# Retention attention in pairs of tiles, with eight tiles of loads ahead

## The chip, the cores and the metric

The kernel runs on one core of a Trainium2 chip. The metric is the device time of one execution in microseconds (us), lower is better; the time before is 1463.5 us, the median of three runs between 1459.63 and 1469.09. The core has five engines that run their own queues of instructions in order: TensorE (PE, matmuls and weight loads), VectorE (DVE), ScalarE (ACT), GpSimd (POOL) and SyncE (SP, which mostly issues DMAs). ACT and POOL issue DMAs too.

## The reference

```python
# _attn_ref: 8 batches, 8 heads, 576 positions, head size 64
scores = scale * np.matmul(q, k.transpose(0, 1, 3, 2))
Dmat = np.where(rel >= 0, gamma[:, None, None] ** rel[None, :, :], 0.0)
return np.matmul(scores * Dmat[None, :, :, :], v)
...
# _moe_ref: x is the attention's output as 4608 rows of 512
logits = x @ w_gate + modality_bias[modality_id]
e_idx = np.argmax(logits, axis=1)
...                                   # gate_w: softmax weight of the chosen expert
out[mask] = gate_w[mask, None] * (np.maximum(x[mask] @ w1[e], 0.0) @ w2[e])
...
# _moe2_ref
h = x @ w_in
return (h - np.tanh(h)) @ w_out
```

## The kernel before

The work has three stages: attention with routing (the first 165 us or so), the experts, and the second feed-forward layer. The change touches only the first, and the place in SBUF of the second layer's weights.

**Attention.** The 4608 rows are cut into 36 tiles of 128 rows. A batch has 576 rows, so nine tiles (PERIOD) hold two batches, and the fifth tile of nine holds the end of one and the start of the next. Within a tile all pairs of positions are computed with a mask; what comes from earlier tiles of the same batch goes through a running state. Per tile there are four groups of matmuls on PE, and each uses the array in another form, which the rows show as partitions of input x output: the scores, keys times queries (L301, 64*128); the state times the queries (L337, 64*64); the values times the masked scores (L345, 128*64); and the keys times the values, added to the state (L360, 128*64). Tiles without an earlier one in their batch have no state-times-query.

**Around it.** DVE multiplies the scores by the mask (L305, two instructions a tile, each frees one of three PSUM banks `sc`) and takes the sum `xp` out of PSUM with the decay factors `gx` (L370). ACT copies the state out (L364), POOL scales the values (L311, `vs`). `attend` does the last three matmul groups of a tile; the loop over t issues the scores of tile t+1 first, then `attend(t)`, `evac_x(t)`, the scaling of tile t+2, and the loads of tile t+4 (AHEAD is 4). SP issues the loads `qk` and `vk`, 512 KB each; a load waits until its buffer's last reader is done.

**Routing.** Four tiles make a group. In the group's next four tiles the loop does `route_a` (gate matmuls, L401, and a copy on ACT, L404), `route_b` (four transposes, L410, and seven small DVE instructions), and `route_c` (rank matmuls, L435 to L440, then on DVE the positions from L443 and the gate to L453), one in each tile. Each tile also stores an older one: `turn_x` transposes it on PE (L468, four transposes, written `turn` below), ACT multiplies it by the gate (L473, `xo`) and issues the DMA to `x_d` (L474). POOL scatters the token numbers (L457). All of these use two PSUM banks with the name `m`; a group of matmuls that needs the third waits until the reader of the first is done. `xo` has two buffers as well, each free when its DMA has landed.

**The end of the stage.** After group 6 `due` doubles the stores of its tiles, `choose` (L376) picks the first expert, SP loads that expert's token numbers, POOL gathers its rows, PE turns them (L148), and the first expert matmul is L630.

Of the kernel before, what the change touches and what calls it, by code (L numbers as in the profile page):

```python
# [8 lines left out]
F32 = mybir.dt.float32  # L9
F32R = mybir.dt.float32r  # L10
# [4 lines left out]
ALU = mybir.AluOpType  # L15
# [9 lines left out]
TL = 128  # L25
NTILE = NT // TL
PERIOD = 9
AHEAD = 4
RG = 4
NRG = NTILE // RG  # L30
UE = 400
# [70 lines left out]
def kernel(tc, A, out):  # L102
    nc = tc.nc
    with ExitStack() as ctx:
# [9 lines left out]
        tok_d = dram.tile([NT + UE, 1], I32, name="tok_d")  # L114
        wo_d = dram.tile([F3, 128, DM], F32, name="wo_d")
        keep = pool("keep", 1)
        wres = pool("wres", 1)

        ident = keep.tile([128, 128], F32, name="ident")
        winh = wres.tile([128, F3, DM], F32R, name="winh")  # L120
        winl = wres.tile([128, F3, DM], F32R, name="winl")

        xT_p = [pool("xTa", 1), None]
        idt0 = keep.tile([128, SE], I32, name="idt0")
        pick = keep.tile([1, 2], I32, name="pick")
# [74 lines left out]
        with tc.manual_schedule():  # L200
# [3 lines left out]
            p1, p1r = pools(c1), pools(c1r)  # L204
            att = p1("att", 1)
            gld = p1("gld", AHEAD)
            tmp = p1("tmp", 2)
            const = p1r("const", 1, side="right")
            xt_p = p1r("xt", 3, side="right")
            xo_p = p1r("xo", 2, side="right")  # L210
# [6 lines left out]
            mask = att.tile([128, 2, TL], F32, name="mask")  # L217
            gx = att.tile([128, PERIOD, H // 2, TL], F32, name="gx")
            vsc = att.tile([128, PERIOD, H], F32, name="vsc")
            state = [att.tile([128, H // 2, D], F32, name=f"state{i}") for i in range(2)]  # L220
            wg = const.tile([128, KD, 32], F32, name="wg")
            ltri = const.tile([128, 128], BF16, name="ltri")
            ones = const.tile([128, 128], BF16, name="ones")
# [21 lines left out]
            def load_gx(r):  # L245
                nc.sync.dma_start(out=gx[:, r], in_=A["gx"][r])
# [11 lines left out]
            nc.scalar.dma_start(out=mb.rearrange("p a e -> p (a e)"), in_=A["mb"].to_broadcast([128, 2 * E]))  # L258
            load_tile(3)
            load_gx(2)  # L260


            nc.gpsimd.memset(ones, 1.0)
# [29 lines left out]
            def scores(t):  # L293

                qk, vk = gt[t]
                a = tmp.tile([128, 2, H // 2, TL], F32, name="a")
                sc = [ps_sc.tile([128, H // 2, TL], F32, name="sc") for _ in range(2)]
                for p in range(H // 2):
                    for s in range(2):
                        r64 = slice(64 * s, 64 * s + 64)  # L300
                        nc.tensor.matmul(out=sc[s][:, p, :], lhsT=qk[r64, 1, p, :], rhs=qk[r64, 0, p, :],  # L301
                                         start=True, stop=True, tile_position=(64 * s, 0))
                m = int(t % PERIOD == PERIOD // 2)
                for s in range(2):
                    nc.vector.tensor_tensor(out=a[:, s], in0=sc[s], in1=mask[:, m:m + 1, :].to_broadcast([128, H // 2, TL]), op=ALU.mult)  # L305
                a_t[t] = a
# [8 lines left out]

            st_box = [None]

            def attend(t):
                qk, vk = gt.pop(t)
                r = t % PERIOD  # L320
                xp = ps_x.tile([128, 2, 4, TL], F32, name="xp")
                a, vs = a_t.pop(t), v_t.pop(t)
                inter = r != 0

                mid_t = r == PERIOD // 2
                after = not inter or mid_t or t == NTILE - 1
                w = TL // 2 if mid_t else TL

                def before():

                    if inter:
                        ss = s_t.pop(t)
                        for p in range(H // 2):
                            for s in range(2):
                                c = s ^ p % 2
                                r64 = slice(64 * s, 64 * s + 64)
                                nc.tensor.matmul(out=xp[64 * c:64 * c + 64, s, p // 2, 0:w], lhsT=ss[r64, p, :], rhs=qk[r64, 0, p, 0:w],  # L337
                                                 start=not after and p < 2, stop=after, skip_group_check=True, tile_position=(64 * s, 64 * c))

                if not after:  # L340
                    before()
                for p in range(H // 2):
                    for s in range(2):
                        c = s ^ p % 2
                        nc.tensor.matmul(out=xp[64 * c:64 * c + 64, s, p // 2, :], lhsT=vs[:, 2 * p + s],  # L345
                                         rhs=a[:, s, p, :], start=after and p < 2, stop=True,
                                         skip_group_check=True, tile_position=(0, 64 * c))
                if after:
                    before()
                x_ps[t] = xp[:, :, 0:2]  # L350
                if r != PERIOD - 1:
                    first = r == 0 or mid_t
                    if first:
                        st_box[0] = ps_st.tile([128, H // 2, D], F32, name="st")
                    st = st_box[0]
                    k0 = TL // 2 if mid_t else 0
                    for p in range(H // 2):
                        for s in range(2):
                            h = 2 * p + s
                            nc.tensor.matmul(out=st[64 * s:64 * s + 64, p, :], lhsT=vk[k0:TL, 1, h * D:(h + 1) * D],  # L360
                                             rhs=vs[k0:TL, h], start=first and p == 0, stop=True, skip_group_check=True,
                                             tile_position=(k0, 64 * s))
                    s_t[t + 1] = state[t % 2]
                    nc.scalar.copy(out=state[t % 2], in_=st)  # L364

            def evac_x(t):
                g, r = divmod(t, RG)
                if r == 0:
                    xt[g] = xt_p.tile([128, KD, RG * TL], F32, name="xt")
                nc.vector.tensor_tensor(out=xt[g][:, :, r * TL:(r + 1) * TL].rearrange("p (s b) t -> p s b t", s=2), in0=x_ps.pop(t),  # L370
                                        in1=gx[:, t % PERIOD].rearrange("p (s b) t -> p s b t", s=2), op=ALU.mult)
# [104 lines left out]
            def store_x(t, spare=False):  # L476
# [4 lines left out]
            scaled(0)  # L481
            scores(0)
            scaled(1)
            bt = xo_p.tile([128, DM], F32, name="xo")
            midf, midn = bt[:, 0:NTILE], bt[:, NTILE:2 * NTILE]
            b1 = bt[:, 2 * NTILE:(2 + E) * NTILE].rearrange("p (t e) -> p t e", e=E)
            nc.gpsimd.tensor_copy(out=midf, in_=mid[:, :, 0])
            nc.gpsimd.tensor_scalar(out=midn, in0=midf, scalar1=-1.0, scalar2=1.0, op0=ALU.mult, op1=ALU.add)
            sh = [128, NTILE, E]
            nc.gpsimd.tensor_tensor(out=bias, in0=midn.unsqueeze(2).to_broadcast(sh),  # L490
                                    in1=mb[:, 0:1, :].to_broadcast(sh), op=ALU.mult)
            nc.gpsimd.tensor_tensor(out=b1, in0=midf.unsqueeze(2).to_broadcast(sh),
                                    in1=mb[:, 1:2, :].to_broadcast(sh), op=ALU.mult)
            nc.gpsimd.tensor_tensor(out=bias, in0=bias, in1=b1, op=ALU.add)
            def due(w):

                r = w - (EARLY - 1) * RG
                return [w][w < 0:] if not 0 <= r < RG else [w + r, w + r + 1] if r < RG // 2 else []

            for t in range(NTILE):  # L500
                g, r = divmod(t, RG)
                if t + 1 < NTILE:
                    scores(t + 1)
                attend(t)
                evac_x(t)
                if t + 2 < NTILE:
                    scaled(t + 2)
                if t + AHEAD < NTILE:
                    load_tile(t + AHEAD)
                if t + 3 < PERIOD:  # L510
                    load_gx(t + 3)
                if t >= RG + 3:
                    for w in due(t - RG - 3):
                        scatter(w)
                if g >= 1:
                    if r == 0:
                        ls_box[g - 1] = route_a(g - 1)
                    elif r == 1:
                        route_b(g - 1, ls_box.pop(g - 1))
                    elif r == 2:  # L520
                        route_c(g - 1)
# [3 lines left out]
                if t == (EARLY + 1) * RG - 1:  # L525
                    choose()
                if t == (EARLY + 1) * RG + 1:
# [83 lines left out]
            t_ahead = late.pop(0)  # L611
            tp_ahead = turn_x(t_ahead, False)
            c1.close()


            def blocks(names, nf, lag, width, xT, load_w, gemm1_w, gemm2, post, prep, finish):
# [341 lines left out]
```

## Time and profile before

| | |
|---|---|
| median of 3 runs | 1463.5 us (1459.63 to 1469.09) |
| profiled execution | 1468.45 us, span 1466.7 us |
| busy over the span | PE 96%, DVE 71%, ACT 47%, POOL 17% |
| busy in 30 to 145 us | PE 115.00 of 115 us, DVE 77.15, ACT 31.76, POOL 55.20 |

Engine times are busy times of one profiled execution. A wait is the idle time of an engine just before an instruction, put down to the work that ended last before it. In rows of the timeline the first column is the start in us, the second the length in us, then engine, line, operation, output and inputs, shape and count, and in square brackets the idle time before. A matmul's row ends later than the next one may start, so the spacing of starts tells what a group takes.

### The profile page before, as it was taken

How to read it: one execution, taken by the hardware profiler on the slowest of the kernel's cores; microseconds unless marked ns; L12 is line 12 of the kernel's file. 1: busy time of each engine (PE TensorE's matmuls, PEld its weight loads, DVE VectorE, ACT ScalarE, POOL GpSimd, SP SyncE). 2: the span in 40 equal slices, each digit the busy share in tenths (PEclk: the TensorE clock that was granted, in tenths of full speed). 3: DMA queues.
4: the chain of work that ended last, by engine and by line, in shares of the span. 5: the costliest groups of instructions: out<-in, count | busy, mean ns of one | idle time of the engine just before them, and what ended most of it. 6: DMA issues, size and time to landing. Idle time of an engine off the chain costs nothing.

```text
span 1466.7 us, 22476 instructions
## 1 busy us (share of the span) xinstructions
PE 1404.4 (96%) x8427; PEld 1214.1 (83%) x8427; DVE 1046.8 (71%) x1745; ACT 683.1 (47%) x1269; POOL 244.8 (17%) x304
## 2 busy tenths in 40 slices
PE   6999689899999999999989999999999999999997
PEld 5888489888999999998768888888888888888885
DVE  2666367877788887438877768777677777778764
ACT  0223144233444444336655555555555555555543
POOL 4455321111111110012420011110011110011101
PEclk8999899999999999999999999999999999999998
DMA  9999354334364443532110000000000010000000
GB/s 331 342 329 327 118 182 130 112 120 109 105 184 93 86 86 98 144 66 59 58 57 1 29 29 29 29 1 31 28 29 29 21 38 1 29 29 0 30 1 29
DMA packets 65490, 130.32 MB, mean 89 GB/s; under 512 B 22288, under 2 KB 29136, under 8 KB 65376
## 3 DMA queue, kind: packets, MB, share of 16 engines
q1 hardware_dynamic: 49168, 91.96, 21.7%
q0 software_dynamic: 7904, 21.96, 4.6%
q10 hardware_dynamic: 8304, 14.91, 2.8%
q8 instruction: 68, 1.11, 0.3%
q14 instruction: 46, 0.38, 0.1%
HBM read 130.97 MB, written 35.61 MB: 114 GB/s over the span
## 4 chain that ended last, share of the span: by engine, by line
PE 42%; issue 6%; DVE 4%; ACT 1%; POOL 1%; DMA 1%; DVEq 0%; POOLq 0%; ACTq 0%
PE hp L630 21%; PE acc L915 7%; PE acc L916 7%; PE acc L917 7%; DVE xl L896 1%; DVE xl L897 1%; DMA o<-wo_d 1%; ACT xh L886 1%; DVE xh L888 1%; DVE xl L895 1%; POOL out_dram L928 0%; DVE lo L891 0%; POOL woutl L869 0%; ACT xh L893 0%; ACT xl L894 0%
## 5 line engine op out<-in xcount | busy, mean ns | idle before, releaser
L915 PE MATMUL acc<-wouth,hi 128*128 128x512 f32 x576 | 226.1, 393 | 4.6 <-ACT o L925 4.6
L630 PE MATMUL hp<-yh,winh 128*128 128x512 f32 x576 | 226.4, 393 | 1.7 <-PEq L851 1.7
L917 PE MATMUL acc<-wouth,lo 128*128 128x512 f32 x576 | 226.1, 393 | 1.7 <-DVE lo L891 1.7
L630 PE MATMUL hp<-yl,winh 128*128 128x512 f32 x576 | 226.2, 393 | 0.0
L630 PE MATMUL hp<-yh,winl 128*128 128x512 f32 x576 | 226.1, 393 | 0.0
L916 PE MATMUL acc<-woutl,hi 128*128 128x512 f32 x576 | 226.1, 393 | 0.0
L885 ACT ACTIVATE xh<-hp 128x512 f32<-128x512 f32 x144 | 86.1, 598 | 297.1 <-PE hp L630 275.4
L887 DVE TENSOR_TENSOR xl<-xh,hp 128x512 f32<-128x512 f32 x144 | 99.0, 688 | 160.6 <-ACT xh L886 160.6
L730 ACT ACTIVATE hi<-hp 128x400 fp32r<-128x400 f32 x96 | 48.4, 505 | 224.8 <-PE hp L630 147.6
L896 DVE SCALAR_TENSOR_TENSOR xl<-xh,xl 128x512 f32<-128x512 f32 x144 | 136.7, 950 | 15.4 <-DVE xl L895 0.5
L830 PE MATMUL acc<-hi,wh 128*128 128x400 f32 x384 | 138.5, 361 | 9.5 <-DVE yo L807 8.6
L832 PE MATMUL acc<-hi,wl 128*128 128x400 f32 x384 | 134.3, 350 | 3.0 <-DVE wl L706 2.6
L630 PE MATMUL hp<-xl,wh 128*128 128x400 f32 x384 | 132.9, 346 | 0.4 <-DVE xl L150 0.4
L915 PEld LDWEIGHTS acc<-wouth,hi 128*128 128x128 f32 x576 | 108.7, 189 | 29.3 <-ACT o L925 5.0
L630 PE MATMUL hp<-xh,wl 128*128 128x400 f32 x384 | 132.7, 345 | 0.2 <-DVE wl L706 0.2
L630 PE MATMUL hp<-xh,wh 128*128 128x400 f32 x384 | 132.3, 345 | 0.2 <-ACT wh L705 0.2
L831 PE MATMUL acc<-lo,wh 128*128 128x400 f32 x384 | 132.4, 345 | 0.0
L917 PEld LDWEIGHTS acc<-wouth,lo 128*128 128x128 f32 x576 | 108.6, 189 | 28.2 <-DVE lo L891 5.2
L630 PEld LDWEIGHTS hp<-yh,winh 128*128 128x128 f32 x576 | 108.3, 188 | 26.2 <-PEq L851 2.0
L630 PEld LDWEIGHTS hp<-yh,winl 128*128 128x128 f32 x576 | 108.1, 188 | 24.8
L916 PEld LDWEIGHTS acc<-woutl,hi 128*128 128x128 f32 x576 | 108.7, 189 | 23.3
L630 PEld LDWEIGHTS hp<-yl,winh 128*128 128x128 f32 x576 | 108.1, 188 | 24.0
(162 smaller groups left out, 2544.2 us busy)
## 6 DMA issues: line engine op xcount, KB each, us to landing
raw<-in_w_dram SPq DMA_DIRECT2D x91, 512.0 KB
qk<-in_qk_dram SPq DMA_DIRECT2D x36, 512.0 KB
vk<-in_vk_dram SPq DMA_DIRECT2D x35, 512.0 KB
y_d<-yo SPq DMA_DIRECT2D x12, 800.0 KB
yr<-y_d SPq DMA_DIRECT2D x9, 1024.0 KB
raw<-in_wo_dram SPq DMA_DIRECT2D x16, 512.0 KB
raw<-in_wi_dram SPq DMA_DIRECT2D x16, 512.0 KB
x_d<-xo ACTq DMA_DIRECT2D x28, 256.0 KB
```

The costliest lines, as they stand in the source:

```text
L630: nc.tensor.matmul(out=hp, lhsT=lhs, rhs=rhs, start=j == 0, stop=j == 3 * KD - 1)
L730: nc.scalar.activation(out=hi, in_=hp, func=ACTF.Relu)
L830: nc.tensor.matmul(out=o, lhsT=wh[:, cs], rhs=hi, start=first, stop=False)
L831: nc.tensor.matmul(out=o, lhsT=wh[:, cs], rhs=lo, start=False, stop=False)
L832: nc.tensor.matmul(out=o, lhsT=wl[:, cs], rhs=hi, start=False, stop=last)
L885: nc.scalar.activation(out=u, in_=hp, func=ACTF.Square)
L886: nc.scalar.activation(out=t, in_=hp, func=ACTF.Tanh)
L887: nc.vector.tensor_tensor(out=v, in0=u, in1=hp, op=ALU.mult)
L896: nc.vector.scalar_tensor_tensor(out=v, in0=s, scalar=SQ_C, in1=v, op0=ALU.add, op1=ALU.mult)
L915: nc.tensor.matmul(out=acc[s], lhsT=hi[:, c], rhs=wouth[f], start=first, stop=False)
L916: nc.tensor.matmul(out=acc[s], lhsT=hi[:, c], rhs=woutl[f], start=False, stop=False)
L917: nc.tensor.matmul(out=acc[s], lhsT=lo[:, c], rhs=wouth[f], start=False, stop=last)
```

## The change

Two tiles go through the loop together. `attend` is split into `keep_state` (keys times values and the copy of the state), `intra` (values times masked scores) and `inter` (state times queries). For a pair t, t+1 the order on PE is: scores of t+2; `keep_state(t)`, `intra(t)`, `intra(t+1)`, `keep_state(t+1)`, `inter(t)`, `inter(t+1)`; then `route_a` where it is due; scores of t+3; then the transposes of two older tiles, with `route_b` between them or `route_c` ahead of them. Both tiles of a pair share one `xp` tile of two banks, and both `evac_x` stand behind the second `inter`. Scaled values and masked scores have four buffers instead of two, the state three instead of two, the loads eight instead of four, and eight tiles of loads are issued ahead of the loop. The POOL work on the routing bias moves behind the scaling of the second pair. The weights `winh` and `winl` get their place in SBUF after attention's buffers are given up instead of ahead of them.

```diff
-AHEAD = 4
+AHEAD = 8
...
-            tmp = p1("tmp", 2)
+            tmp = p1("tmp", 4)
...
-            state = [att.tile([128, H // 2, D], F32, name=f"state{i}") for i in range(2)]
+            state = [att.tile([128, H // 2, D], F32, name=f"state{i}") for i in range(3)]
...
+            for t in range(4, AHEAD):
+                load_tile(t)
+                load_gx(t - 1)
...
-            for t in range(NTILE):
+            for t in range(0, NTILE, 2):
                 g, r = divmod(t, RG)
-                if t + 1 < NTILE:
-                    scores(t + 1)
-                attend(t)
-                evac_x(t)
-                if t + 2 < NTILE:
-                    scaled(t + 2)
...
+                if t + 2 < NTILE:
+                    scores(t + 2)
+                keep_state(t)
+                intra(t)
+                intra(t + 1)
+                keep_state(t + 1)
+                inter(t)
+                inter(t + 1)
+                evac_x(t)
+                evac_x(t + 1)
+                for w in (t + 2, t + 3):
+                    if w < NTILE:
+                        scaled(w)
...
+                if g >= 1 and r == 0:
+                    ls_box[g - 1] = route_a(g - 1)
+                if t + 3 < NTILE:
+                    scores(t + 3)
+                if g >= 1 and r == 0:
+                    out_tiles(t)
+                    route_b(g - 1, ls_box.pop(g - 1))
+                    out_tiles(t + 1)
+                elif g >= 1:
+                    route_c(g - 1)
+                    out_tiles(t)
+                    out_tiles(t + 1)
```

Here `out_tiles` does a tile's scatters and stores. Two places of the order follow. First PE at a tile with the ranks (`route_c`), from one scores to the next; before, where a tile has one store (`sc` scores, `st` keys times values, `m` the shared banks, a bracket names the engine waited for):

```order
L337 MATMUL xp<-qk,state_122 64x128 x7
L345 MATMUL xp<-a,vs 64x128 [waits Pool_49]
L345 MATMUL xp<-a,vs 64x128 x7
L360 MATMUL st<-vs,vk 64x64 [waits DMAHW2_49]
L360 MATMUL st<-vs,vk 64x64 x7
L468 MATMUL m<-ident,xt 128x128 [waits DVE_49]
L468 MATMUL m<-ident,xt 128x128 x3
L301 MATMUL sc<-qk 128x128 [waits DMAHW7_49]
```

That is the tile after the ranks: the bank that the ranks' reader on DVE must free is asked for one whole tile later. The same work in the changed kernel, in the second pair of a group:

```order
L365 MATMUL xp<-qk,state_117 64x128 x8
L365 MATMUL xp<-qk,state_118 64x128 x8
L300 MATMUL sc<-qk 128x128 [waits DMAHW0_49]
L300 MATMUL sc<-qk 128x128 [waits DVE_49]
L300 MATMUL sc<-qk 128x128 x6
...
L442 MATMUL m<-cum,ones 128x32
L470 MATMUL m<-ident,xt 128x128 x4
L470 MATMUL m<-ident,xt 128x128 [waits DVE_49]
L470 MATMUL m<-ident,xt 128x128 x3
L300 MATMUL sc<-qk 128x128 [waits DMAHW2_49]
```

Now the second transpose stands four transposes behind the ranks and waits for DVE. Then DVE around the ranks' reader `rk`; before:

```order
L305 TENSOR_TENSOR a<-sc,mask 128x512 x2
L370 TENSOR_TENSOR xt<-xp,gx 128x4x128
L443 TENSOR_TENSOR rk<-m,ecap 128x32
L444 TENSOR_TENSOR rk<-rk,oh_all 128x32
L446 TENSOR_REDUCE pos_s<-rk 128x4
```

And in the changed kernel:

```order
L304 TENSOR_TENSOR a<-sc,mask 128x512 x2
L372 TENSOR_TENSOR xt<-xp,gx 128x4x128 x2
L304 TENSOR_TENSOR a<-sc,mask 128x512 x2
L445 TENSOR_TENSOR rk<-m,ecap 128x32
L446 TENSOR_TENSOR rk<-rk,oh_all 128x32
```

The reader of the ranks stood behind one evacuation, and now stands behind two evacuations and two masks that come after them.

## Rows read from the trace of the kernel before

**Rows 1.** Windows: busy us (count) by engine, granted PE clock, DMA share, GB/s
```profile
20.00:30.00 10.00, 5.67 (x64) 5.05 (x64) 1.79 (x3) 0.00 (x0) 4.54 (x7) 0.50 1.03 402
30.00:145.00 115.00, 115.00 (x1977) 94.31 (x1975) 77.15 (x192) 31.76 (x65) 55.20 (x77) 0.99 0.94 330
```

**Rows 2.** Timeline of PE alone, one tile from scores to scores
```profile
109.19 0.19 PE L435 MATMUL m<-oh_all,ltri 128*128 128x32 bf16 x1
...
109.33 0.63 PE L468 MATMUL m<-ident,xt 128*128 128x128 f32 x4
109.89 1.16 PE L301 MATMUL sc<-qk 64*128 64x128 f32 x16
110.98 0.67 PE L337 MATMUL xp<-qk,state 64*64 64x128 f32 x16
111.58 1.09 PE L345 MATMUL xp<-a,vs 128*64 128x128 f32 x16
112.50 0.64 PE L360 MATMUL st<-vs,vk 128*64 128x64 f32 x16
113.07 0.66 PE L468 MATMUL m<-ident,xt 128*128 128x128 f32 x4
113.66 0.38 PE L301 MATMUL sc<-qk 64*128 64x128 f32 x2
```

**Rows 3.** Waits in the first 200 us: us, times, longest
```profile
PE sc L301 <- DMA qk<-in_qk_dram: 10.1, 2, 5.7
PE xp L345 <- POOL vs L311: 4.0, 1, 4.0
PE m L376 <- ACT xo L473: 3.6, 1, 3.6
```

**Rows 4.** Waits of SP's DMA queue, first 200 us
```profile
SPq L241 <- PE xp L337: 57.5, 25, 3.7
SPq L242 <- PE st L360: 29.8, 20, 4.4
```

**Rows 5.** Timeline, tiles 30 and 31 and the stores behind them
```profile
141.48 1.09 PE L468 MATMUL m<-ident,xt 128*128 128x128 f32 x8
...
141.67 0.19 DVE L443 TENSOR_TENSOR rk<-m,ecap 128x32 f32<-128x32 f32 x1
...
142.50 0.97 PEld L301 LDWEIGHTS sc<-qk 64*128 64x128 f32 x16 [0.17 <-issue]
...
143.70 1.29 DVE L305 TENSOR_TENSOR a<-sc,mask 128x512 f32<-128x512 f32 x2
143.74 0.69 ACT L473 ACTIVATE xo<-m,gate 128x512 f32<-128x512 f32 x1 [1.90 <-DVE se L451]
144.46 0.33 ACTq L474 DMA_DIRECT2D x_d<-xo  x1
...
149.50 0.69 ACT L473 ACTIVATE xo<-m,gate 128x512 f32<-128x512 f32 x1 [2.79 <-DMA x_d<-xo]
150.22 0.33 ACTq L474 DMA_DIRECT2D x_d<-xo  x1
150.24 0.17 PE L376 MATMUL m<-cum,ones 128*128 128x8 bf16 x1 [3.59 <-ACT xo L473]
```

**Rows 6.** Groups by line, first 200 us: busy us, mean ns, idle before
```profile
L370 DVE TENSOR_TENSOR xt<-xp,gx 128x512 f32<-128x512 f32 x36 | 24.8, 690 | 25.7 <-PE xp L345 14.3 <-remote 7.7 <-DMA gx<-in_gx_dram 2.9
L473 ACT ACTIVATE xo<-m,gate 128x512 f32<-128x512 f32 x28 | 19.1, 683 | 23.5 <-DVE se L452 7.4 <-DMA x_d<-xo 6.1 <-PE sc L301 3.8
```

**Rows 7.** Timeline at the end of the stage, last tile to first expert
```profile
165.53 0.67 PE L337 MATMUL xp<-qk,state 64*64 64x128 f32 x16
...
174.93 0.69 DVE L370 TENSOR_TENSOR xt<-xp,gx 128x512 f32<-128x512 f32 x1 [7.68 <-remote]
...
180.02 0.45 PE L630 MATMUL hp<-xh,wh 128*128 128x400 f32 x1 [0.23 <-ACT wh L705]
```

More of the change, by code (lines that the diff above doesn't have):

```diff
@@ L116 @@
         keep = pool("keep", 1)
-        wres = pool("wres", 1)
         ident = keep.tile([128, 128], F32, name="ident")
-        winh = wres.tile([128, F3, DM], F32R, name="winh")
-        winl = wres.tile([128, F3, DM], F32R, name="winl")
         xT_p = [pool("xTa", 1), None]
@@ L316, with intra @@
             st_box = [None]
[L318 to L341, printed above, removed]
+            xps = [None]
+            def intra(t):
+                if t % 2 == 0:
+                    xps[0] = ps_x.tile([128, 2, 4, TL], F32, name="xp")
+                xp = xps[0][:, :, 2 * (t % 2):2 * (t % 2) + 2]
+                a, vs = a_t.pop(t), v_t[t]
                 for p in range(H // 2):
@@ L345, in attend, with keep_state @@
                         nc.tensor.matmul(out=xp[64 * c:64 * c + 64, s, p // 2, :], lhsT=vs[:, 2 * p + s],
-                                         rhs=a[:, s, p, :], start=after and p < 2, stop=True,
+                                         rhs=a[:, s, p, :], start=t % 2 == 0 and p < 2, stop=True,
                                          skip_group_check=True, tile_position=(0, 64 * c))
-                if after:
-                    before()
-                x_ps[t] = xp[:, :, 0:2]
+                x_ps[t] = xp
+            def keep_state(t):
+                vk, vs = gt[t][1], v_t[t]
+                r = t % PERIOD
+                mid_t = r == PERIOD // 2
                 if r != PERIOD - 1:
@@ L362, in attend, with inter @@
                                              tile_position=(k0, 64 * s))
-                    s_t[t + 1] = state[t % 2]
-                    nc.scalar.copy(out=state[t % 2], in_=st)
+                    s_t[t + 1] = state[t % 3]
+                    nc.scalar.copy(out=state[t % 3], in_=st)
+            def inter(t):
+                qk = gt.pop(t)[0]
+                v_t.pop(t)
+                if t not in s_t:
+                    return
+                ss = s_t.pop(t)
+                w = TL // 2 if t % PERIOD == PERIOD // 2 else TL
+                for p in range(H // 2):
+                    for s in range(2):
+                        c = s ^ p % 2
+                        r64 = slice(64 * s, 64 * s + 64)
+                        nc.tensor.matmul(out=x_ps[t][64 * c:64 * c + 64, s, p // 2, 0:w], lhsT=ss[r64, p, :], rhs=qk[r64, 0, p, 0:w],
+                                         start=False, stop=True, skip_group_check=True, tile_position=(64 * s, 64 * c))
             def evac_x(t):
@@ L483, with make_bias @@
             scaled(1)
[L484 to L494, printed above, removed]
+            scores(1)
+            def make_bias():
+                bt = xo_p.tile([128, DM], F32, name="xo")
+                midf, midn = bt[:, 0:NTILE], bt[:, NTILE:2 * NTILE]
+                b1 = bt[:, 2 * NTILE:(2 + E) * NTILE].rearrange("p (t e) -> p t e", e=E)
+                nc.gpsimd.tensor_copy(out=midf, in_=mid[:, :, 0])
+                nc.gpsimd.tensor_scalar(out=midn, in0=midf, scalar1=-1.0, scalar2=1.0, op0=ALU.mult, op1=ALU.add)
+                sh = [128, NTILE, E]
+                nc.gpsimd.tensor_tensor(out=bias, in0=midn.unsqueeze(2).to_broadcast(sh),
+                                        in1=mb[:, 0:1, :].to_broadcast(sh), op=ALU.mult)
+                nc.gpsimd.tensor_tensor(out=b1, in0=midf.unsqueeze(2).to_broadcast(sh),
+                                        in1=mb[:, 1:2, :].to_broadcast(sh), op=ALU.mult)
+                nc.gpsimd.tensor_tensor(out=bias, in0=bias, in1=b1, op=ALU.add)
             def due(w):
@@ L498, in due, with out_tiles @@
                 return [w][w < 0:] if not 0 <= r < RG else [w + r, w + r + 1] if r < RG // 2 else []
-            for t in range(NTILE):
-                g, r = divmod(t, RG)
-                if t + 1 < NTILE:
-                    scores(t + 1)
-                attend(t)
-                evac_x(t)
-                if t + 2 < NTILE:
-                    scaled(t + 2)
[L508 to L511, printed above, removed]
+            def out_tiles(t):
                 if t >= RG + 3:
@@ L514 @@
                         scatter(w)
[L515 to L521, printed above, removed]
+                if t >= RG:
                     for w in due(t - RG - 2):
@@ L524 @@
                             store_x(w)
-                if t == (EARLY + 1) * RG - 1:
+            for t in range(0, NTILE, 2):
+                g, r = divmod(t, RG)
+                if t + 2 < NTILE:
[11 more added lines that the diff above has]
+                        scaled(w)
+                if t == 2:
+                    make_bias()
+                for w in (t, t + 1):
+                    if w + AHEAD < NTILE:
+                        load_tile(w + AHEAD)
+                    if w + AHEAD - 1 < PERIOD:
+                        load_gx(w + AHEAD - 1)
+                if g >= 1 and r == 0:
[10 more added lines that the diff above has]
+                    out_tiles(t + 1)
+                if t + 1 == (EARLY + 1) * RG - 1:
                     choose()
-                if t == (EARLY + 1) * RG + 1:
+                if t == (EARLY + 1) * RG:
                     base = nc.sync.value_load(pick[0:1, 0:1], min_val=0, max_val=(E - 1) * CAP)
@@ L613 @@
             c1.close()
+            wres = pool("wres", 1)
+            winh = wres.tile([128, F3, DM], F32R, name="winh")
+            winl = wres.tile([128, F3, DM], F32R, name="winl")
             def blocks(names, nf, lag, width, xT, load_w, gemm1_w, gemm2, post, prep, finish):
```

## The prediction, made before the changed kernel ran

> **What bounds the kernel now.** Three stages follow each other, and the change lies in the first, so I read the windows of that stage, then PE's timeline, then the waits. Between 30 and 145 us PE is busy all the time, with DVE at two thirds and ACT at a quarter [rows 1]. PE hardly waits for data there: in the whole stage it waits twice for a load, 10.1 us in all, once for the scaled values, 4.0 us, all before 30 us [rows 3]. The loads wait for PE instead: SP stood 57.5 us for the readers of `qk` and 29.8 us for those of `vk` [rows 4]. So PE's own order sets the pace, and a deeper queue of loads meets no wait in that stretch. The DMA share is 0.94 there [rows 1]; if that is a real limit, a faster PE could gain at most 0.06 x 115 = 6.9 us before loads became the bound.
>
> "Busy" hides something in PE's row. One tile takes 113.66 - 109.89 = 3.77 us [rows 2], in five groups of matmuls with four changes of the array's form: 64\*128, 64\*64, 128\*64 twice (values, then state), 128\*128. A transpose group of four takes 113.66 - 113.07 = 0.59 us of that tile. Eight transposes in a row take 1.09 us [rows 5] where four take 0.66 [rows 2], so four without a change cost 0.43. The difference, 0.16 us, is my price of one change of form; the bounds are 0 (the gap belongs to a wait that every group has) and 0.17, the idle time of the weight-load row of the next scores [rows 5].
>
> The Trainium skill has two rules on such gaps. "TensorEngine Tiling (Array Packing)", section Tiling Modes, says that a change of tiling mode drains TensorE; by that rule the pairing saves what I count below. "Perfetto Trace Analysis", section Identifying Performance Opportunities, says that the same gap repeating on the engine that should be saturated can mean too few buffers in SBUF or PSUM; by that rule the gaps stay, which is rival 3.
>
> **The change, part by part.**
> - *Forms.* Two tiles had eight changes. The new order (scores, state, values twice, state, state-times-query twice, scores, transposes) has five. Three fewer in each of 15 pairs that also store or nearly so: 45 x 0.16 = 7.2 us less (0 to 7.7).
> - *The ranks' bank.* In the second pair of each group the ranks take one of the two `m` banks, the first transpose the other, and the second transpose needs the ranks' bank back. DVE frees it after two evacuations (2 x 0.69 [rows 6]), two masks (1.29 [rows 5]) and the reader itself (0.19 [rows 5]): 2.86 us after the last state-times-query. PE gets there after a change (0.16), the scores (109.89 to 110.98, 1.09), the ranks (109.19 to 109.33, 0.14) and one transpose group (0.43): 1.82 us [rows 2]. PE waits 1.04 us, seven times: 7.3 us more. If DVE takes the first evacuation 0.44 us earlier it is 0.6 (4.2 us); with 0.3 us of hand-overs 1.3 (9.4 us). Before, a whole tile lay between. Behind PE in that wait stands everything of the next pair.
> - *The scaling's bank.* In the first pair of a group the second transpose needs the bank that ACT's scaling of the first one frees. ACT takes 0.68 us [rows 6] plus the tail of a matmul, about 0.66 - 0.43 = 0.2; only the four transposes of `route_b` lie between, 0.43. That is 0.45 us, six times: 2.7 us more (0 to 4).
> - *The gate.* From the ranks' reader (141.67) to the end of the scaling that needs the gate (143.74 + 0.69) it is 2.76 us [rows 5]. The state copy of the next pair stands behind two such scalings on ACT, and the second `keep_state` waits for it. It comes about in time; I take 1 us in all (0 to 4).
> - *Four stores at once.* At tiles 30 and 31 four tiles are stored, now in one pair. The third transpose waits for the first's scaling, which waits for the gate: 2.67 + 2.76 = 5.4 us after the last state-times-query, where PE arrives at 2.86 + 0.43 = 3.3. That is 2.1 us more (0 to 3). The wait of `choose`, 3.59 us behind the scaling that waits for a store's DMA [rows 5], stays.
> - *The start.* Up to 25 us the order of the loads is the same. The clock was 0.50 between 20 and 30 us, and the DMA share was 1.03 at 402 GB/s [rows 1], so earlier issue brings nothing there. The 4.0 us wait for scaled values [rows 3] goes, since POOL's bias work moves behind them; in its place PE waits for the scores' data of tile 4, which the new order asks for before it works on tile 2. I take 0, bounds -4 and +4.
> - *The end of the stage.* The last pair adds nothing; the first weights of the expert no longer wait for the last evacuation. But the last state-times-query starts at 165.53, and the evacuation that needs it at 174.93 after 7.68 us of idle time whose releaser the profile doesn't name; the first expert matmul is at 180.02 [rows 7]. No row tells why. I leave this wait as it is (0), and its going is rival 2. The place of `winh` and `winl` in SBUF costs nothing: they are written long after, in the experts' stage.
>
> Transferred bytes, DVE's and ACT's work and the number of matmuls are unchanged. The sum is -7.2 + 7.3 + 2.7 + 1.0 + 2.1 = +5.9 us. After the stage PE is nearly full to the end, so the shift goes through. Against the profiled execution, 1468.45 us, that is 1474; the profiled one is 5 us above the median of the three runs, and against the median I forecast 1463.5 + 5.9, about **1470 us**.
>
> **The rivals.**
> 1. *The banks come free in time.* If DVE takes the ranks' reader before PE gets there, only the fewer changes are left: -7.2 + 1.0 = -6, some 1457 us, at most the 6.9 us that the DMA share leaves. For it: DVE has a third of its time free [rows 1]. Against it: the order on DVE is fixed, and the masks need the scores that PE has just done.
> 2. *The unexplained wait at the hand-over goes.* It is 7.7 us [rows 7], and nothing in the program's order demands it. With the rest as forecast: 1470 - 7.7 = 1462 us; with rival 1 as well: 1457 - 7.7 = 1449, the only case I see near 1% faster.
> 3. *The gaps are waits, not forms.* Then the 7.2 us don't come: 1470 + 7 = 1477 us. Against it: between values and state, which have one form, PE starts the state 0.92 us after the values, no more than those take, though both sides wait on semaphores [rows 2].
> 4. *The slower side: the stores.* `xo` has two buffers, and a store took about 149.50 - 144.46 = 5.0 us from its issue to the next use of its buffer, with 2.79 us of waiting [rows 5]. Now two stores go out together, the gate-held ones at about 5.5 us after the last state-times-query; the next pair's first store wants the buffer 8.2 + 2.9 - 5.5 = 5.6 us later (a pair's time, then the gate matmuls, scores and one transpose). Four loads in a burst share the DMA engines with them. Up to 5.6 us nothing happens; at 7 us ACT waits 1.4 us six times and 2 us at `choose`, PE's transposes behind it: 1470 + 10 = 1480 us.
>
> **How the numbers follow.** The forecast has a chance of 0.50, with its own range of 1463 to 1477 from the bounds of the waits. Rival 1 has 0.20, rival 2 alone 0.08 and with rival 1 0.04, rival 3 0.06, rival 4 0.12. About 1% (14.6 us) is what a measurement of this kernel tells from no change: faster means below 1449, slower above 1478. Slower takes most of rival 4, part of rival 3 and a little of the forecast's upper end, 0.17. Faster is rivals 1 and 2 together, and a bit for what I don't see, 0.06. The rest, 0.77, is no change. The range goes from rival 1 with a gain of 8 us at the start or the end to rival 4 with a little more, 1455 to 1482 us.
>
> **What the profile after would show.** Right: on PE's timeline, starts of the four groups of a pair with fewer gaps; among the waits a new row, transposes into `m` waiting for DVE's ranks' reader, about 1 us seven times, and for ACT's scaling, about 0.5 us six times; SP waiting for PE as before; the last state-times-query some 5 to 8 us later than 165.5. Wrong: no such wait rows and an earlier end (rival 1); the evacuation of the last tile right behind its matmuls (rival 2); a tile's time in the stretch without route work still 3.8 us (rival 3); ACT's scaling waiting for `x_d` DMAs in most groups (rival 4). PE waiting for `qk` or `vk` after 35 us would break the first part: then loads, not PE, set the pace.

## The result, and the profile after

The changed kernel takes **1470.7 us** (median of 6 runs, 1466.9 to 1475.2), the kernel before beside it 1463.2 us; the ratio is 1.0058, with a 95% interval of 1.0036 to 1.0079. The forecast was 1470. The total was right by luck: the profile shows that two errors cancel in it. Attention lost 16.5 us where 5.9 were forecast, and the hand-over to the experts, forecast to stay as it was, became 9 us shorter. The profiled execution has a span of 1473.0 us, 6.3 more than before.

The same window of the changed kernel (columns as in [rows 1]):

```profile
30.00:145.00 115.00, 102.77 (x1726) 84.94 (x1724) 63.28 (x163) 26.74 (x55) 49.50 (x71) 0.98 0.88 322
```

PE, busy for all of the 115 us before [rows 1], now stands idle for 12.2 of them, at nearly the same clock (0.98 after 0.99) and with DMA less busy (0.88 after 0.94): PE waits more, and in that window not for loads (the four waits in the first row below all lie before 30 us). The longest waits of PE, and ACT's wait for its stores, in the first 200 us (us in all, times, longest):

```profile
PE sc L300 <- DMA qk<-in_qk_dram: 14.7, 4, 5.5
PE m L470 <- ACT xo L475: 6.6, 7, 2.0
ACT xo L475 <- DMA x_d<-xo: 6.4, 6, 2.0
PE m L470 <- DVE rk L445: 6.3, 7, 0.9
```

The second and the fourth row are the two that the prediction named. PE's timeline through the second pair of a group shows how they arise:

```profile
86.83 1.10 PE L365 MATMUL xp<-qk,state 64*64 64x128 f32 x32
87.86 1.16 PE L300 MATMUL sc<-qk 64*128 64x128 f32 x16
...
89.09 0.64 PE L470 MATMUL m<-ident,xt 128*128 128x128 f32 x4
90.63 0.66 PE L470 MATMUL m<-ident,xt 128*128 128x128 f32 x4 [0.91 <-DVE rk L445]
91.22 1.16 PE L300 MATMUL sc<-qk 64*128 64x128 f32 x16
```

Two state-times-query groups in a row take 87.86 - 86.83 = 1.03 us, where one with a change of form behind it took 0.60 [rows 2]: 2 x 0.60 - 1.03 = 0.17 for a change. The two turns take 91.22 - 89.09 = 2.13 us where eight transposes take 1.09 [rows 5]: 1.04 us too long, and the same wait of 0.9 us stands in all seven second pairs with ranks. Both are the prices of the forecast. What it did not have is in the first pair of the group (POOL, PE and ACT in one timeline):

```profile
75.95 1.01 POOL L459 DMA_INDIRECT slot_d<-tokid,pos_s  x1 [0.16 <-DMA vk<-in_vk_dram]
...
76.39 0.32 PE L365 MATMUL xp<-qk,state 64*64 64x128 f32 x1
...
76.56 0.23 PE L347 MATMUL st<-vs,vk 64*64 64x64 f32 x2
76.62 1.01 PE L365 MATMUL xp<-qk,state 64*64 64x128 f32 x26
76.95 0.12 POOL L458 MEMSET nopt<- 128x1 f32 x1
77.26 0.96 POOL L459 DMA_INDIRECT slot_d<-tokid,pos_s  x1 [0.18 <-issue]
78.01 0.34 PE L365 MATMUL xp<-qk,state 64*64 64x64 f32 x3 [0.39 <-issue]
78.05 0.37 ACT L351 COPY state<-st 128x256 f32<-128x256 f32 x1 [2.08 <-PE xp L365]
...
78.28 1.58 PE L403 MATMUL m<-xt,wg 128*32 128x512 f32 x8
```

From the first state-times-query (76.39) to the gate matmuls it is 1.9 us in place of 1.03, and ACT's copy of the state, whose matmuls were done by 76.8, begins at 78.05. In that time POOL carried two indirect DMAs in a row (scatters of token numbers), 0.3 us apart with a small memset between. I call such a delay of what waits for PE a hold, and indirect DMAs that follow each other so closely a row of them. At the end of the stage the 7.68 us wait of [rows 7] is not there: the evacuation follows its matmuls, and the first expert matmul comes 5.5 us after the last state-times-query (14.5 before); 8.3 of the 9.0 us lie between that group's start and its evacuation (1.1 us where it was 9.4):

```profile
182.03 1.11 PE L365 MATMUL xp<-qk,state 64*64 64x128 f32 x29 [0.46 <-issue]
...
183.17 1.29 DVE L372 TENSOR_TENSOR xt<-xp,gx 128x512 f32<-128x512 f32 x2 [3.26 <-PE xp L365]
...
187.56 0.45 PE L657 MATMUL hp<-xh,wh 128*128 128x400 f32 x1 [0.37 <-ACT wh L732]
```

Where the 16.5 us went, by the starts of scores in the two timelines (before, after): from tile 8 to 16, 46.0 to 77.9 and 44.0 to 82.9, 7.0 us more, with 2.0 gained ahead of it; from 16 to 32, 64.6 and 72.7, 8.1 more; from 32 to the last state-times-query, 23.0 and 26.4, 3.4 more.

### The profile page after: what moved, and what is told of

Read it like the earlier page. It is cut to its first block, busy times and chain, and to the rows that moved or that the text cites. A ratio compares the mean times of both kernels' runs of the same rounds, so it can differ in the third digit from the quotient of the medians.

```text
span 1473.0 us, 22454 instructions
## 1 busy us (share of the span) xinstructions
PE 1408.9 (96%) x8427; PEld 1221.4 (83%) x8427; DVE 1041.7 (71%) x1745; ACT 683.4 (46%) x1269; POOL 245.2 (17%) x304
## 4 chain that ended last, share of the span: by engine, by line
PE 42%; issue 6%; DVE 4%; ACT 1%; POOL 1%; DMA 1%; DVEq 0%; POOLq 0%; ACTq 0%
PE hp L657 21%; PE acc L942 7%; PE acc L943 7%; PE acc L944 7%; DVE xl L923 1%; DVE xl L924 1%; DMA o<-wo_d 1%; ACT xh L913 1%; DVE xh L915 1%; DVE xl L922 1%; POOL out_dram L955 0%; DVE lo L918 0%; POOL woutl L896 0%; ACT xh L920 0%; ACT xl L921 0%
```

## The experiments

Comments in the diffs are mine and not in the kernels.

**The kernel before again** (one run, 1470.0 us).

> The kernel before, unchanged, profiled once more. The question is the 7.7 us idle of DVE (and the same of ACT) between the last state-times-query and the last evacuation, which the first profile of it shows and that of the changed kernel does not. Theory A, the wait belongs to this order of work: it comes back at the same place, 6 to 9 us long, and the first expert matmul starts 13 to 15 us after the last state-times-query. Theory B, the wait is an accident of one execution (or of recording it): it is gone or stands elsewhere, the first expert matmul comes 5 to 7 us after the last state-times-query, near 172 us, and the profiled span is some 1460 us.

The wait at the hand-over is 7.9 us again, from a state-times-query at 166.41 to its evacuation at 175.88. It came in both profiles of this kernel: it belongs to the kernel, not to one execution.

**The ranks first.** Edit to the changed kernel:

```diff
+                if g >= 1 and r != 0:
+                    rk_box = route_c(g - 1)      # rank matmuls and their first reader
                 if t + 3 < NTILE:
                     scores(t + 3)
...
-                    route_c(g - 1)
+                    route_d(g - 1, *rk_box)      # the rest of route_c
```

> The changed kernel with one move: the rank matmuls and their first reader on DVE stand ahead of the scores of tile t+3 (and so ahead of two masks on DVE) instead of behind them; the rest of the routing stays where it is. Theory A, the wait of the second transpose for the ranks' bank is a loss of its own: the seven waits of 0.9 us go, one more change of form in seven pairs comes in (7 x 0.16 = 1.1 us), and the time falls by 5 us against the changed kernel, to about 1465. Rival, PE would wait at the next place anyway (gate-held scalings, or instructions that are not there): the rows move, and the time stays within 2 us of 1470.

Measured 1474.1 us, ratio 1.0071 (1.0042 to 1.0099): no gain where 5 us were expected. The wait for the ranks' reader has gone from the list, and in its place stand:

```profile
PE m L475 <- ACT xo L480: 8.5, 7, 3.1
PE st L347 <- ACT state L351: 3.6, 4, 1.4
```

Second pairs (mean of four, tile 16 to 32) went from 7.96 to 7.23 us, first pairs from 10.22 to 11.01. PE comes to the next pair earlier, and there meets the gate-held scalings on ACT and POOL's two DMAs, as far as the rows tell; the shares of the two are not separated. "Perfetto Trace Analysis" in the Trainium skill, section Identifying Performance Opportunities, lets a repeated gap mean too few buffers; here reordering alone took the gap away, and the time did not follow.

**Four buffers for the stores.** Edit: `xo_p = p1r("xo", 4, ...)` in place of 2.

> The changed kernel with four buffers for the scaled rows that are stored (xo) instead of two, so that ACT does not wait for a store's DMA. Theory A: the two long stops of PE at 59 and 98 us (1.7 and 1.4 us, behind a scaling that waits for a store) and the slow clock that follows the first (about 1.6 us) go, and at the four stores in one pair 1 us: 4 to 5 us less than the changed kernel, about 1466. Rival: these stops are ACT waiting for PE's own work, and four buffers change nothing, 1470.

Measured 1469.7 us, ratio 1.0033 (1.0015 to 1.0052): by the ratios 3.7 us below the changed kernel, near the 4 to 5 expected, but the two intervals overlap. ACT's wait for `x_d` is gone. In the changed kernel it had stopped PE (ACT and PE in one timeline):

```profile
59.50 0.66 PE L412 MATMUL m<-ident,ls 128*128 128x128 f32 x4 [0.19 <-ACT ls L406]
61.43 0.69 ACT L475 ACTIVATE xo<-m,gate 128x512 f32<-128x512 f32 x1 [1.99 <-DMA x_d<-xo]
62.17 0.66 PE L470 MATMUL m<-ident,xt 128*128 128x128 f32 x4 [2.02 <-ACT xo L475]
```

and the clock had fallen right behind it:

```profile
62.86:66.27 3.41, 3.41 (x40) 3.19 (x42) 1.29 (x2) 1.06 (x2) 0.00 (x0) 0.51 0.89 348
```

With four buffers PE keeps full clock there, and tiles 8 to 16 take 35.6 us where they took 38.9.

**Only the deeper loads.** Edit to the kernel before: `AHEAD = 8`, its loads, and the late place of `winh` and `winl`; tiles one by one.

> The kernel before with the loads alone: eight tiles of loads ahead instead of four, and the weights' place in SBUF given later (the room needs it); tiles still one by one. Theory A, PE's own order sets the pace and loads never did: the time stays within 2 us of 1463, and between 30 and 145 us PE is busy all the time as before. Rival, deeper loads help or harm by themselves: more than 3 us away from 1463, by loads that arrive before PE asks (faster) or by bursts of loads that hold up the stores (slower, with rows of ACT's scaling waiting for store DMAs).

Measured 1465.7 us, ratio 1.0012 (0.9996 to 1.0027): without pairs, no gain. In its profile the last state-times-query starts earlier (162.59, 165.53 before), but its evacuation again waits 7.9 us without a named releaser, and PE then waits 3.0 us for the expert's weights, whose loads SP issues only after PE has turned the gathered rows; the first expert matmul starts at 180.48 (180.02 before).

**Only the pairs.** Edit to the changed kernel: `AHEAD = 4`.

> The changed kernel with four tiles of loads ahead, where it has eight. Theory A: the deeper loads move nothing, the pairing alone makes the difference: 1470.7 us within 2. Rival F: bursts of two tiles' loads that run far ahead hold the stores back; with four ahead ACT's waits for x_d are gone and the time is 1467 to 1469 us. Rival G: with only two pairs of loads ahead PE waits for qk or vk: slower than 1474 us.

Measured 1483.8 us, ratio 1.0109 (1.0081 to 1.0138): slower, as the last of the three theories had it. By the starts of scores the time goes at both ends of the stage: tile 8 comes 4.0 us later than in the changed kernel, and from tile 32 to the last state-times-query it is 6 us more. Two rows of PE's timeline show a wait in each, for a load at the start and for the four stores ahead of the choice (0.51 us in the changed kernel); why the stores are later with fewer loads ahead is not shown:

```profile
37.90 1.16 PE L300 MATMUL sc<-qk 64*128 64x128 f32 x16 [2.36 <-DMA qk<-in_qk_dram]
...
173.24 0.17 PE L378 MATMUL m<-cum,ones 128*128 128x8 bf16 x1 [3.22 <-ACT xo L475]
```

The pace from tile 16 to 32 is that of the changed kernel, 72.5 us.

**Why PE's work counts as done late.** All halts of PE, DVE and ACT over 0.3 us between 30 and 187 us whose releaser the profiles of the two kernels don't name overlap with indirect DMAs of POOL, or end within 1.1 us behind one; the longest lie where several stand in a row. At the hand-over of the kernel before there are eight (first, fifth and last of them on POOL, and ACT's cast, which waited for PE):

```profile
163.52 1.01 POOL L158 DMA_INDIRECT vk<-x_d,idt  x1 [2.12 <-issue]
...
168.52 1.02 POOL L457 DMA_INDIRECT slot_d<-tokid,pos_s  x1 [0.19 <-issue]
...
172.39 0.95 POOL L457 DMA_INDIRECT slot_d<-tokid,pos_s  x1 [0.19 <-issue]
...
174.99 1.07 ACT L149 CAST xh<-sc 128x512 fp32r<-128x512 f32 x2 [9.70 <-remote]
```

They end at 173.34, and what waited for PE, DVE's evacuation [rows 7] and ACT's cast, starts at 174.93 and 174.99. The events of PE's semaphore, by which it tells the other engines that a group is done, show the same for the whole stage: of 56 updates that fell due inside such a DMA, 30 came over 0.3 us after the end of their matmul's row; of 159 others, 5. (17 of the 56 have no event of their own and are counted with the next.) "Perfetto Trace Analysis" in the Trainium skill, section Tensor Engine Instruction (MATMUL, LD_WEIGHTS), says that the profile's end of a matmul is an estimate and that its semaphore update is pushed and propagated after it; here a row ended at 166.20, and its update came at 174.91. Whether POOL's DMAs put it off is what the next runs test.

**Scatters apart.** Edit to the changed kernel, first pairs only:

```diff
                 for w in (t + 2, t + 3):
                     if w < NTILE:
                         scaled(w)
+                    if r == 0:
+                        slots(w - 2)             # the scatter, taken out of out_tiles
```

> The changed kernel with POOL's order altered in the first pair of each group: scaled values, one scatter, scaled values, one scatter, where it had both scaled values and then two scatters in a row. Theory C: while POOL carries out an indirect DMA (0.95 to 1.01 us), PE's semaphore updates arrive late, and two in a row hold them 1.2 to 2.1 us, with PE's state-times-query of that pair behind them (2.07 to 2.28 us for 32 matmuls where 1.03 is usual). Then the late updates fall to about 1 us at most, the six groups go back to about 1.0 us, the last state-times-query comes 4 to 6 us earlier than 182.0, and the time is about 1466 us (1464 to 1468). Rival D: the halts are PE's instruction packets behind bursts of loads. Then they stay and the time is 1470 to 1471 us.

Measured 1471.2 us, ratio 1.0038 (1.0020 to 1.0055), above the expected time. In the first pairs the holds went as expected (POOL, PE and ACT in one timeline):

```profile
74.48 1.01 POOL L459 DMA_INDIRECT slot_d<-tokid,pos_s  x1 [0.16 <-issue]
...
75.52 1.05 POOL L310 TENSOR_TENSOR vs<-vk,vsc 128x512 f32<-128x512 f32 x1
...
76.14 0.84 PE L365 MATMUL xp<-qk,state 64*64 64x128 f32 x29
76.36 0.37 ACT L351 COPY state<-st 128x256 f32<-128x256 f32 x1 [0.86 <-PE st L347]
...
76.77 1.01 POOL L459 DMA_INDIRECT slot_d<-tokid,pos_s  x1 [0.16 <-issue]
...
76.91 1.06 PE L403 MATMUL m<-xt,wg 128*32 128x512 f32 x8
```

First pairs fell from 10.22 to 9.34 us, and tiles 16 to 32 took 69.2 us. But then the four gathers, which come earlier here, held PE in the last pair, so that the last state-times-query is only 2.0 us earlier, and the time was missed (the ratio fell by 0.002, less than the intervals tell apart):

```profile
169.40 1.10 PE L365 MATMUL xp<-qk,state 64*64 64x128 f32 x32
...
172.93 0.86 POOL L154 DMA_INDIRECT vk<-x_d,idt  x1 [0.30 <-issue]
174.79 1.29 DVE L372 TENSOR_TENSOR xt<-xp,gx 128x512 f32<-128x512 f32 x2 [7.88 <-PE sc L300]
```

**Scatters by twos in the kernel before.** Edit: the scatters of tiles 0 to 23 at every second tile, two at a time.

> The kernel before, its scatters of tiles 0 to 23 issued by twos, at every second tile; all else as before. Theory C: PE's updates around the twos are 1.2 to 2.1 us late where single ones make them 0.4 to 1.1 us late. Before has slack for about 1.3 us between a tile's state and the next tile's state-times-query, so each of the 12 twos costs 0 to 0.8 us: time 1464 to 1474 us, most likely 1469. Rival D: the same number of scatters, no other transfer: the time of before within 1 us and no late updates.

Measured 1466.6 us, ratio 0.9998 (0.9983 to 1.0012). The hold comes, but small (POOL and PE in one timeline):

```profile
80.42 1.01 POOL L457 DMA_INDIRECT slot_d<-tokid,pos_s  x1 [0.15 <-issue]
...
81.73 0.96 POOL L457 DMA_INDIRECT slot_d<-tokid,pos_s  x1 [0.18 <-issue]
...
82.35 0.46 PE L360 MATMUL st<-vs,vk 128*64 128x64 f32 x6
83.19 0.54 PE L360 MATMUL st<-vs,vk 128*64 128x64 f32 x10 [0.38 <-issue]
```

Tiles 16 to 32 took 66.9 us in place of 64.6. My 5 us were too many: unpaired tiles have slack for most of a hold. The whole time does not show the rest; in this profile the half clock of 148.4 to 155.3 (granted clock 0.51 there in the kernel before) did not come, and the last state-times-query started at 165.35.

**The last scatters held back in the kernel before.** Edit:

```diff
                     for w in due(t - RG - 3):
-                        scatter(w)
+                        if w < NTILE - 2 * RG:
+                            scatter(w)
...
             def rest_a():
-                for i in range(3):
-                    scatter(NTILE - RG - 3 + i)
+                nc.gpsimd.tensor_copy(out=nopt, in_=ls_last[:, 0:1])
+                for i in range(4):
+                    scatter(NTILE - RG - 4 + i)
```

> The kernel before, with the scatters of tiles 28 to 31 held back on POOL by a copy that reads the last group's turned scores, so that only the four gathers stand in a row at the hand-over (163.5 to 168.2) and not eight indirect DMAs (to 173.3). Theory C: PE's updates of the last tile come by 169 to 170 and not at 174.9, the evacuation of the last tile follows there, the first expert matmul starts at 174 to 176 where it was 180.0, and the time is 4 to 6 us below the kernel before. Rival E: the 7.7 us wait belongs to something else at the hand-over (the clock, the gather's data, a buffer): it stays, and the time is that of before within 1 us.

Measured **1460.1 us**, ratio 0.9962 (0.9939 to 0.9986), 5.6 us below before. The evacuation starts 4.0 us after its matmuls start (9.4 in [rows 7]), behind the last gather, and the first expert matmul 9.8 us earlier than in [rows 7]; 3.9 of these are the stage's own earlier end, since the half clock of 148.4 to 155.3 did not come in this execution (in the next run, with a like gain, it did), so 5.9 are left for the hand-over:

```profile
161.65 0.67 PE L337 MATMUL xp<-qk,state 64*64 64x128 f32 x16
...
163.66 0.86 POOL L158 DMA_INDIRECT vk<-x_d,idt  x1 [0.30 <-issue]
...
165.62 0.69 DVE L370 TENSOR_TENSOR xt<-xp,gx 128x512 f32<-128x512 f32 x1 [2.97 <-PE sc L148]
...
170.18 0.45 PE L632 MATMUL hp<-xh,wh 128*128 128x400 f32 x1 [1.23 <-ACT wh L707]
```

**Gaps between the scatters in the kernel before.** Edit: a 128x512 product on a spare tile of POOL ahead of each of the same four scatters, which keep their place.

> The kernel before with about 1 us of other POOL work (a 128x512 product on a tile of its own) ahead of each of the scatters of tiles 28 to 31 at the hand-over; their number and order are as before, and POOL is busy with them longer, to about 178 us. Theory C in its narrow form: only indirect DMAs with no gap between them hold PE's updates; in the first gap, right after the four gathers, they get through. Then the last tile's evacuation starts 9 us earlier relative to its state-times-query than in before, within 2 to 4 us, the first expert matmul is at 171 to 175 us, and the time is 4 to 6 us below before. Rival H: as long as any of these DMAs is still to be carried out, the updates stay away. Then the wait grows to about 12 us and the time is 3 to 5 us above before.

Measured **1458.4 us**, ratio 0.9951 (0.9933 to 0.9970). PE's updates get through in the first gap, with four DMAs still to come:

```profile
163.78 0.86 POOL L158 DMA_INDIRECT vk<-x_d,idt  x1 [0.31 <-issue]
164.66 1.06 POOL L459 TENSOR_TENSOR gap<-gap 128x512 f32<-128x512 f32 x1
...
165.75 0.69 DVE L372 TENSOR_TENSOR xt<-xp,gx 128x512 f32<-128x512 f32 x1 [2.07 <-PE sc L148]
...
165.92 1.06 POOL L461 DMA_INDIRECT slot_d<-tokid,pos_s  x1 [0.16 <-issue]
...
170.83 0.70 PE L634 MATMUL hp<-xh,wh 128*128 128x400 f32 x1
```

So it is the row without a gap that holds PE, not how many DMAs are still to come. What in the row does it (POOL's own work, or the transfers that it starts) is not separated, nor how short a gap would do: the DMAs of a row are 0.3 us apart, and that was too little.

**Both mends in the kernel before.** Edit: the scatters held back, and four buffers for `xo`.

> The kernel before with the scatters of tiles 28 to 31 held back as in the run that was 5.6 us faster, and four buffers for the stores' rows where it has two. Before, ACT waits 6.1 us for x_d stores in all, and PE 3.6 us for ACT ahead of the choice, with half clock behind it (148.4 to 155.3). Expected if those waits cost what they show: 2 to 4 us below the run with the scatters held back alone, 1456 to 1458 us. Rival: the choice then waits for the gate instead, and the half clock comes later: 1460 us.

Measured **1453.9 us**, ratio 0.9920 (0.9890 to 0.9950), more than expected (its interval overlaps with that of the scatters held back alone). It beats both kernels, with tiles one by one. PE's wait ahead of the choice is 0.6 us (3.6 in [rows 3]), and the half clock behind it is gone.

**The pairs mended.** Edit to the changed kernel: scatters apart, four buffers for `xo`, the gap between gathers, and

```diff
-                if t + 2 < NTILE:
+                if t + 2 < NTILE and t != 2:     # at t == 2 behind the pair's work
                     scores(t + 2)
...
+                if g >= 1 and r == 0:
+                    out_tiles(t)                 # the first turn, ahead of the scores
                 if t + 3 < NTILE:
                     scores(t + 3)
```

> The changed kernel with each cause mended that the runs have shown or the prediction named, but for the ranks' bank: scatters apart in the first pairs, four buffers for the stores' rows, the first turn ahead of the second scores (no wait for the scaling's bank), scores of tile 4 behind the work on tile 2, and 1 us of other POOL work between the four gathers. Terms: the six holds 0.8 us each, the scaling's bank 6 x 0.5, the stores 1.5 + 1.4, the start 2 to 4, the gathers 2: in all 12 to 15 us less attention, the last state-times-query at 168 to 171 us where it was 182, and the time 1460 to 1463 us. Rival: the pairs' waits move to the gate (as in the run with the ranks first) or the start's loads, and less than half of it comes: 1465 to 1469 us.

Measured **1458.4 us**, ratio 0.9957 (0.9941 to 0.9973), a little below the expected 1460 to 1463: some 14.8 us below the changed kernel by the two ratios. First pairs take 8.59 us, tiles 16 to 32 66.2, the last state-times-query starts at 167.8, the first expert matmul at 173.34. Apart from the loads of the first 35 us (13.8 us), the longest waits of PE up to the last state-times-query are down to

```profile
PE m L472 <- DVE rk L447: 6.3, 7, 0.9
PE m L472 <- ACT xo L477: 1.4, 1, 1.4
PE xp L367 <- ACT state L353: 0.7, 1, 0.7
```

**The holds alone.** Edit to the changed kernel: scatters apart, and the gap between gathers.

> The changed kernel with the scatters of the first pairs apart, as in the run of that name, and about 1 us of other POOL work between the four gathers; nothing else. In that run the holds of the first pairs had gone, but the gathers, which came 7 us earlier there, held PE for about 3.6 us between 170.4 and 176.6. Theory C: with gaps this goes too, the last state-times-query is at 176 to 178 us (182.0 in the changed kernel, 180.0 with the scatters apart alone), and the time is 5 to 7 us below the changed kernel: ratio to before 1.001 to 1.002. Rival: what the holds cost is given back at the choice or the gather's end, and the ratio stays at 1.004.

Measured 1469.4 us, ratio 1.0072 (1.0046 to 1.0097), beside runs of the kernel before that were lower (1460.6) than those beside the other experiments. By the profile it came nearly as expected up to the last pair: the last state-times-query at 178.30, the first expert matmul at 183.43, 4.1 us ahead of the changed kernel's. By the ratio nothing was gained, and its interval overlaps with that of the changed kernel. What removing the holds alone is worth in the whole time of the pairs stays open; it is shown for the kernel before (5.6 and 6.4 us) and, together with the other mends, for the pairs.

## Why the prediction was right, and where it was not

- **Forms.** Right: 0.17 us by the direct row, 0.16 forecast. (The values and the state share one form, 128\*64 in [rows 2], as the prediction counts and unlike what the section on the kernel before says.) Rival 3 falls with it; the section Tiling Modes of the Trainium skill's "TensorEngine Tiling (Array Packing)", cited in the prediction, agrees with the row.
- **The ranks' bank.** Right in place, number and size: seven times 1.04, so rival 1 falls. That it was repairable was no use (the ranks first): by the rows the next waits, for the gate-held scaling and the state copy, took over.
- **The scaling's bank.** Right in size: from `route_b` to the second turn 0.9 us, for 0.43 of work. Twice it was the store that held the scaling (2.02 us at 62.17), rival 4's mechanism, in two groups and not in six. Four buffers took it away.
- **Four stores at once.** The third turn waits 1.39 us (2.1 forecast); the third and fourth together then take 2.77 us (165.20 to 167.97) for 0.87 of work at full clock; the granted clock was 0.50 from 165.3 to 172.1. But the wait of the choice, which I left at 3.59 [rows 5], is 0.51: in all about 0.2 us where I had 2.1.
- **The start.** 2.0 us gained by tile 8, inside the bounds; but profiles of the kernel before and of its variants with the same order at the start reach tile 8 anywhere from 42.0 to 47.0 us, so one pair of profiles doesn't tell this gain. "A deeper queue of loads meets no wait" holds for single tiles, but not for pairs: without it their ratio is 0.005 higher.
- **Not in the sum: POOL's order.** The change moved the scatters so that two stand in a row in each first pair. I had counted POOL's busy time and not the order of its DMAs. The holds are 0.9 of the 1.5 us that first pairs lost beyond the forecast: in a group of four tiles 16.67 us were forecast (16.14 - 6 x 0.16 + 1.04 + 0.45), 18.18 measured, 17.31 with the scatters apart.
- **Failed: "I leave this wait as it is (0)".** The wait of [rows 7] was the same hold, by eight DMAs in a row; breaking the row in two ways took most of it away (4.0 and 3.8 us from the start of the matmuls to the evacuation, 9.4 before). In the changed kernel the last group's scatters wait for the ranks (185.28) and leave the row, so the wait goes. That is rival 2, to which I gave 0.12 in all, and its sign, the evacuation right behind its matmuls, stands in the profile beside the forecast's own. The prediction said that nothing in the program's order demands the wait; the order on POOL did.

So the total was right by luck: 10.6 us of attention that the sum did not have, by the rows the holds, the store stops and the half clock behind one of them, were nearly paid for by the wait that went (9.0 us). With these mended, tiles 16 to 32 cost 66.2 us in pairs and 64.6 one by one: fewer forms pay for no more than the ranks' bank, as the forecast's first two terms say (-7.2 and +7.3), and 1.6 us are left over.

## What to carry to other kernels

When a change moves work on POOL's queue, write down the order of its indirect DMAs: two or more only 0.3 us apart put off what others see of PE's results, and a microsecond of other POOL work between them lets it through. A wait in the profile whose releaser has long been done is worth an experiment of its own before the change is costed; here removing it from the kernel before gave 5.6 and 6.4 us, while the change itself cost 7.5. And a saving on PE counts only if the next wait in line (bank, gate, store) does not come with the new order.

## What the runs showed of the hardware that I had not expected

- Around a single indirect DMA of POOL (0.95 to 1.0 us) PE's semaphore updates came up to 1.2 us late, around two in a row 1.2 to 1.8, around four 4.3 us (with the scatters apart, a state-times-query that ended at 170.50 was evacuated from 174.79 on), around eight 8.7 (166.20 to 174.93). One 1.06 us instruction in between ended it. Why is not shown.
- A halt of PE of 2.02 us was followed by a stretch of 3.4 us at a granted clock of 0.51, so that it cost nearly twice its length. The length of the halt alone does not tell: with four buffers for the stores, halts of 0.91 and 1.39 us (before 158.03 and 160.07) were followed by 6.8 us at 0.50, while the clock stayed at 1.00 behind 1.70 us before 100.63 in the changed kernel and behind 2.55 us before 148.61 with the last scatters held back.
